# Window attention with its gradients: the order of products in a pair of tiles, and the shape of the first scores

## The chip, the cores and the metric

The kernel runs on one core of a Trainium2 chip. The metric is the device time of one execution in microseconds; smaller is better. PE is the matrix engine, DVE the vector engine, ACT the scalar engine, POOL and SP two more engines that here only issue transfers (DMA).

## The reference

The input is an image of 256 x 256 positions with C = 384 channels, cut into 32 x 32 windows of 8 x 8 = 64 positions. Attention is done inside each window, with one head, and a vector-Jacobian product follows:

```python
qkv = xw @ wqkv                       # xw: 1024 windows x 64 x 384
p = softmax(einsum('bqc,bkc->bqk', q, k) * C ** -0.5)
o = einsum('bqk,bkc->bqc', p, v) @ wo
# outputs: o, and the gradients of x, wqkv and wo for a given grad_out
```

All is bfloat16 in memory. The outputs are `out_0` (o), `out_1` (gradient of x), `out_2` and `out_3` (gradients of the weights).

## The kernel before, in words

The weights are folded once at the start into four 384 x 384 matrices, so that the scores and their gradient, and all that follows, are products with x and grad_out directly. A *tile* is 16 x 8 positions, two windows one above the other, 128 rows for the 128 partitions. Four tiles make a *quad*; there are 128 quads, and a call of `step` works on three of them at once: c (the one before), b (this one) and a (the next one).

Accumulators of PE live in one ring of eight slots (`ring`, 8 banks of 128 x 384 or 128 x 512 float32). Each new accumulator takes the slot of the one eight before it, and its first product waits until that slot has been emptied by a copy or an addition on ACT or DVE. The one exception is the scores' tile `sd`, which is held longer. Slots are handed out in the order in which the code asks for them, and the order of instructions on every engine is the order of the code: nothing is rescheduled. The waits are set by the framework from the tiles.

What a step puts on PE, in order:

1. `scores` of b (sd, 24 products of 128 x 128 weights by 64 columns, through `product`, L146).
2. `uv` of b: eight accumulators pj of three products each (128x128 by 384 columns, L146), copied by ACT (L228).
3. `project` kind 0 of a: three accumulators pj of three products (128x128 by 512 columns, L146), copied by ACT (L160).
4. One accumulator pg of a gradient of the weights (`filler(1)`, `gf_group`, twelve products by 384 columns), which DVE adds to `GF_acc` (L289). The products are there from the time that three quads are done.
5. `attend` of c for the tiles 2 and 3, then `turn` of b (pt: eight products of 128 x 64 weights by 128 columns, L234, copied by DVE at L237).
6. `project` kind 1 of a and one more pg, both in column halves: with `split[0]` set, `product` makes two products of 128x64 (L144) that run side by side, one to the lower and one to the upper 64 partitions.
7. `attend` of b for the tiles 0 and 1.

`attend` takes a *pair* of tiles. For each tile it has four accumulators: po (the output), pu and pw (for the gradients of the weights) and pd (gradient of x). `both` makes four 64x64 products for two of these accumulators, which run side by side on the four quarters of the array (L256): first a group of four for pu and po, then a group for pw and pd. So a pair has four groups. After them come, for each tile, two *token products* into pd (K = 128, 128x64 by 384 columns, L271), which use the transposed projections `tok`. po is copied by ACT to osb (L263), pu and pw by DVE to Uq and Wq (L264, L266), and pd by ACT to dsb (L274). `store` issues two transfers per result on POOL's queue (L246). POOL's queue also issues the loads of grad_out (dq, L118), SP's queue the loads of x (xq, L117) and the three transposing transfers of a quad (dT and xT at L127, tok at L166). The loads are issued three quads ahead, the transposes into dT and xT two.

Of the kernel before, what the change touches and what calls it, by code (L numbers as in the profile page):

```python
# [12 lines left out]
F32 = mybir.dt.float32  # L13

P = 128
# [7 lines left out]
def kernel(  # L23
# [21 lines left out]
    nc = tc.nc  # L45
    _, H, W, C = x.shape
# [13 lines left out]
    ring = ctx.enter_context(tc.tile_pool(name="ring", bufs=8, space=bass.MemoryType.PSUM))  # L60
# [26 lines left out]
    for dst, left, lo, right, ro, sc in (  # L87
# [5 lines left out]
        for mr in range(CK):  # L93
            pc = ring.tile([P, C], F32, tag="r")
            for mc in range(CK):
                nc.tensor.matmul(pc[:], lhsT=left[:, lo + mc, mr * P:(mr + 1) * P], rhs=right[:, ro + mc, :],  # L96
                                 start=(mc == 0), stop=(mc == CK - 1))
# [8 lines left out]
    def dram_tile(ap, bp, t):  # L106
        return ap[0, 2 * WIN * bp:2 * WIN * (bp + 1), WIN * t:WIN * (t + 1), :]

    LO, HI = slice(0, WT), slice(WT, P)
# [29 lines left out]
    split = [ALL]  # L139

    def product(out, lhsT, rhs, start, stop):
        if split[0]:
            for h in (LO, HI):
                nc.tensor.matmul(out[h], lhsT=lhsT[:, h], rhs=rhs, start=start, stop=stop)  # L144
        else:
            nc.tensor.matmul(out, lhsT=lhsT, rhs=rhs, start=start, stop=stop)  # L146

    ENG = {"D": nc.vector.tensor_copy, "A": nc.scalar.copy}
# [20 lines left out]
    def scores(st):  # L169
        yz, xT = st["yz"], st["xT"]  # L170
        st["sd"] = sd = ring.tile([P, QUAD, 2, WT], F32, tag="r", name="sd")
        for t in range(QUAD):
            for w in range(2):
                for m in range(CK):
                    product(sd[:, t, w, :], yz[:, m, t, 2 * w:2 * w + 2, :].rearrange("p s k -> p (s k)"),
                            xT[:, t, m, w * WT:(w + 1) * WT], m == 0, m == CK - 1)
# [53 lines left out]
    def turn(st):  # L230
        pt = ring.tile([P, QUAD, 2, WT], F32, tag="r", name="pt")
        for t in range(QUAD):
            for w, h in ((0, LO), (1, HI)):
                nc.tensor.matmul(pt[h, t, :, :].rearrange("p s k -> p (s k)"), lhsT=st["ps"][:, w, t, :],  # L234
                                 rhs=ident[:], start=True, stop=True)
        st["PS"] = dst = qp.tile([P, QUAD, 2, WT], BF16, tag="PS", name="PS")
        nc.vector.tensor_copy(out=dst[:], in_=pt[:])  # L237

    def turned(st, n, t, h):
        if n in ("PT", "ST"):  # L240
            return st["PS"][h, t, int((n == "ST") == (h == LO)), :]
        return st[n][h, t, :]

    def store(dst, src, bp, t):
        for h, w in ((LO, 1), (HI, 0)):
            nc.gpsimd.dma_start(out=dram_tile(dst, bp, t)[WIN * w:WIN * (w + 1)], in_=src[h, :])  # L246

    def attend(st, pair, after=None):
        bp, t0 = st["at"]
        if pair[0] == 0:  # L250
            st["Uq"] = grp.tile([P, QUAD, C], BF16, tag="Uq", name="Uq")
            st["Wq"] = grp.tile([P, QUAD, C], BF16, tag="Wq", name="Wq")
        def both(straight, crossed):
            for h, o, (dst, lhs, rhs, done) in ((LO, LO, straight), (LO, HI, crossed), (HI, LO, crossed),
                                                (HI, HI, straight)):
                nc.tensor.matmul(dst[o, :], lhsT=turned(st, lhs, t, h), rhs=st[rhs][h, t, :], start=True, stop=done)  # L256

        made = []
        for t in pair:
            po, pu, pw, pd = [ring.tile([P, C], F32, tag="r", name=n) for n in ("po", "pu", "pw", "pd")]  # L260
            both((pu, "ST", "xq", True), (po, "PT", "uq", True))
            osb = ob.tile([P, C], BF16, tag="o")
            ENG[EV["o"][t]](out=osb[:], in_=po[:])  # L263
            ENG[EV["U"][t]](out=st["Uq"][:, t, :], in_=pu[:])  # L264
            both((pw, "Pb", "dq", True), (pd, "ST", "vq", False))
            ENG[EV["W"][t]](out=st["Wq"][:, t, :], in_=pw[:])  # L266
            made.append((t, pd))
            store(out_0, osb, bp, t0 + t)
        for t, pd in made:
            for w, o in ((0, HI), (1, LO)):  # L270
                nc.tensor.matmul(pd[o, :], lhsT=st["ps"][:, w, t, :], rhs=st["tok"][:, :, t, w, :], start=False,  # L271
                                 stop=True)
            dsb = ob.tile([P, C], BF16, tag="d")
            ENG[EV["d"][t]](out=dsb[:], in_=pd[:])  # L274
            store(out_1, dsb, bp, t0 + t)
        if after is not None:
            turn(after)
# [22 lines left out]
    def step(c, b, a):  # L300


        def on(st):
            return (lambda f, *r: f(st, *r)) if st is not None else (lambda f, *r: None)
        C_, B, A = on(c), on(b), on(a)
        B(scores)
        B(soft, 0)
        B(uv, 0, 0)
# [17 lines left out]
        if c is not None:  # L326
            attend(c, (2, 3), b)
        else:
            B(turn)
# [4 lines left out]
        filler(1)  # L334
        split[0] = ALL
        B(attend, (0, 1))

    G_ON_PE = 0
    EV = {"z": "AAA", "y": "AAA", "u": "AAAA", "v": "AAAA", "o": "AAAA", "U": "DDDD", "W": "DDDD", "d": "AAAA"}
    quads = [(bp, t0) for bp in range(NBP) for t0 in range(0, NT, QUAD)]  # L340
    sts = [{"at": q, "i": i} for i, q in enumerate(quads)]
    n = len(sts)
# [33 lines left out]
    for ma in range(CK):  # L376
        for i, (lhs, f, rhs, r0) in enumerate(((GFT, 0, w_sb, C), (GFb, 0, w_sb, 0), (GFT, 1, woT_sb, 0))):
            pe = ring.tile([P, C], F32, tag="r")
            for mb in range(CK):
                nc.tensor.matmul(pe[:], lhsT=lhs[:, f, mb, ma * P:(ma + 1) * P], rhs=rhs[:, mb, r0:r0 + C],  # L380
                                 start=(mb == 0), stop=(mb == CK - 1))
# [6 lines left out]
    for mc in range(CK):  # L388
        pe = ring.tile([P, C], F32, tag="r")
        for ma in range(CK):  # L390
            nc.tensor.matmul(pe[:], lhsT=w_sb[:, ma, 2 * C + mc * P:2 * C + (mc + 1) * P], rhs=GFb[:, 1, ma, :],
                             start=(ma == 0), stop=(ma == CK - 1))
# [32 lines left out]
```

## Time and profile before

| what | value |
|---|---|
| median of four runs | 2046.67 us |
| lowest and highest run | 2041.24, 2060.6 us |
| the profiled execution | 2041.24 us, its span 2039.5 us |
| mean granted PE clock | 0.999 |
| copy of po on ACT (L263), mean | 483 ns, 512 of them |
| copy of pd on ACT (L274), mean | 483 ns, 512 of them |
| copies of pu and pw on DVE (L264, L266), mean | 547 and 546 ns, 512 each |
| addition of pg on DVE (L289), mean | 557 ns, 258 of them |
| issue of a store on POOL (L246), mean | 570 and 563 ns, 1024 of each output |
| stores, issue to landing | 4.7 us, median |

A line of a group reads: line of the source, engine, operation, destination and sources, tile shape of the weights (rows*columns), shape of the moving operand, count. In the timeline the first two columns are start and duration in microseconds; instructions of a kind that follow each other are merged, with their number at the end (x8), and brackets tell the idle time before and what ended it. PE's durations run past the start of the next product, because products are pipelined.

### The profile page before, as it was taken

The page shows a single profiled execution, that of the slowest core. Times are in us where ns is not written, and L with a number is a line of the kernel's source. Part 1 is how long each engine was busy: PE and PEld are TensorE (multiplying, and loading weights), DVE is VectorE, ACT ScalarE, POOL GpSimd, SP SyncE. Part 2 cuts the span into 40 slices and gives each one's busy share as a digit, 9 for nine tenths or more (in the row PEclk, how much of TensorE's full clock was granted, in tenths as well). Part 3 has the DMA queues.
Part 4 walks back from the last instruction along what each step waited for, and adds up shares of the span by engine and source line. Part 5 has one row for each costly group of instructions (what it writes and reads, how often), then busy time and mean ns, then how long its engine had stood idle before and what let it go on. Part 6 is the DMA issues. An engine that isn't in the chain of part 4 may idle for free.

```text
span 2039.5 us, 54462 instructions
## 1 busy us (share of the span) xinstructions
PE 2021.9 (99%) x20442; PEld 1146.7 (56%) x20442; DVE 1382.2 (68%) x3107; ACT 1469.3 (72%) x3213; POOL 1419.2 (70%) x2566
## 2 busy tenths in 40 slices
PE   8999999999999999999999999999999999999998
PEld 4455555555555555555555555555555555555555
DVE  5666666666666676666666666666666667666665
ACT  6777777777777777777777777777777777777773
POOL 4766777677666777677676677767666777776764
PEclk9999999999999999999999999999999999999999
DMA  9999999999999999999999999999999999999992
GB/s 208 223 209 198 212 201 203 209 200 213 196 204 194 209 204 212 202 204 202 203 209 200 199 208 202 205 205 202 196 198 213 200 204 202 211 197 204 205 181 79
DMA packets 997192, 409.25 MB, mean 201 GB/s; under 512 B 880704, under 2 KB 971584, under 8 KB 996928
## 3 DMA queue, kind: packets, MB, share of 16 engines
q1 hardware_dynamic: 873648, 253.80, 76.1%
q0 software_dynamic: 122880, 151.68, 31.7%
q8 instruction: 159, 2.61, 0.6%
q14 instruction: 105, 0.86, 0.2%
q10 hardware_dynamic: 400, 0.29, 0.0%
HBM read 101.84 MB, written 101.84 MB: 100 GB/s over the span
## 4 chain that ended last, share of the span: by engine, by line
PE 97%; DMA 1%; DVE 1%; ACT 1%; POOL 0%; issue 0%; POOLq 0%
PE pj L146 36%; PE pg L146 12%; PE pj L144 12%; PE pg L144 12%; PE pd L271 6%; PE pu L256 5%; PE sd L146 5%; PE pw L256 4%; PE pd L256 3%; PE pt L234 1%; DMA dT<-dq 0%; PE pc L96 0%; DMA out_dram<-osb 0%; DMA w_sb<-in_wqkv_dram 0%; PE pe L380 0%
## 5 line engine op out<-in xcount | busy, mean ns | idle before, releaser
L246 POOL DMA_DIRECT2D out_dram<-osb x1024 | 577.1, 570 | 341.5 <-ACT osb L263 145.2
L246 POOL DMA_DIRECT2D out_dram<-dsb x1024 | 571.2, 563 | 207.6 <-DMA dq<-in_grad_out_dram 60.9
L289 DVE TENSOR_TENSOR GF_acc<-pg,GF_acc 128x384 f32<-128x384 f32 x258 | 143.7, 557 | 460.8 <-PE pg L144 316.6
L146 PEld LDWEIGHTS <-xT 128*128 128x128 bf16 x3072 | 291.8, 98 | 182.2
L263 ACT CAST osb<-po 128x384 bf16<-128x384 f32 x512 | 220.9, 483 | 232.6 <-PE pu L256 175.0
L146 PE MATMUL pj<-B_sb,xT 128*128 128x384 bf16 x1536 | 333.4, 326 | 0.0
L146 PE MATMUL pj<-AT_sb,xT 128*128 128x384 bf16 x1536 | 333.3, 326 | 0.0
L118 POOL DMA_DIRECT2D dq<-in_grad_out_dram x512 | 274.1, 550 | 50.2 <-DMA out_dram<-osb 19.4
L228 ACT CAST uq<-pj 128x384 bf16<-128x384 f32 x512 | 247.4, 483 | 73.6 <-PE pj L146 69.4
L264 DVE CAST Uq<-pu 128x384 bf16<-128x384 f32 x512 | 280.0, 547 | 9.5 <-PE pu L256 6.1
L266 DVE CAST Wq<-pw 128x384 bf16<-128x384 f32 x512 | 279.8, 546 | 0.0
L146 PE MATMUL pj<-dT,BT_sb 128*128 128x512 bf16 x1152 | 270.8, 380 | 2.2 <-DMA dT<-dq 2.2
L144 PE MATMUL pj<-xT,A_sb 128*64 128x512 bf16 x2304 | 270.0, 379 | 0.0
L228 ACT CAST vq<-pj 128x384 bf16<-128x384 f32 x512 | 250.1, 489 | 2.4
L274 ACT CAST dsb<-pd 128x384 bf16<-128x384 f32 x512 | 221.2, 483 | 37.7 <-DMA out_dram<-dsb 1.9
L162 ACT CAST yz<-pj 128x512 bf16<-128x512 f32 x384 | 224.6, 586 | 32.0 <-PE pj L144 0.2
L256 PE MATMUL pw<-dq,Pb 64*64 64x384 bf16 x1024 | 228.4, 329 | 0.3
L144 PEld LDWEIGHTS <-xq 128*64 128x64 bf16 x3000 | 170.1, 110 | 86.6
L146 PEld LDWEIGHTS <-xq 128*128 128x128 bf16 x1572 | 153.7, 98 | 115.1 <-issue 0.6
L256 PEld LDWEIGHTS <-PS 64*64 64x64 bf16 x3072 | 120.2, 105 | 163.0 <-issue 150.3
L206 ACT COPY ps<-Pb 64x256 bf16<-64x256 bf16 x256 | 103.2, 403 | 149.6 <-DVE Pb L203 148.1
L160 ACT CAST yz<-pj 128x512 bf16<-128x512 f32 x384 | 206.6, 644 | 2.1 <-PE pj L146 2.0
(64 smaller groups left out, 2720.4 us busy)
## 6 DMA issues: line engine op xcount, KB each, us to landing
xq<-in_x_dram SPq DMA_DIRECT2D x512, 96.0 KB, 4.1
dq<-in_grad_out_dram POOLq DMA_DIRECT2D x512, 96.0 KB, 5.3
out_dram<-osb POOLq DMA_DIRECT2D x1024, 48.0 KB, 4.7
out_dram<-dsb POOLq DMA_DIRECT2D x1024, 48.0 KB, 4.7
dT<-dq SPq DMA_TRANSPOSE x128, 6.0
xT<-xq SPq DMA_TRANSPOSE x128, 7.7
tok<-yz SPq DMA_TRANSPOSE x128, 8.7
w_sb<-in_wqkv_dram SPq DMA_DIRECT2D x1, 864.0 KB, 5.5
```

The costliest lines, as they stand in the source:

```text
L118: nc.gpsimd.dma_start(out=dq[:, t, :], in_=dram_tile(grad_out, bp, t0 + t))
L144: nc.tensor.matmul(out[h], lhsT=lhsT[:, h], rhs=rhs, start=start, stop=stop)
L146: nc.tensor.matmul(out, lhsT=lhsT, rhs=rhs, start=start, stop=stop)
L160: ENG[EV["z"][mo]](out=yz[:, mo, :, 0:4:3, :], in_=pj[:])
L162: ENG[EV["y"][mo]](out=yz[:, mo, :, 1:3, :], in_=pj[:])
L228: cp(out=dst[:, t, :], in_=pj[:])
L246: nc.gpsimd.dma_start(out=dram_tile(dst, bp, t)[WIN * w:WIN * (w + 1)], in_=src[h, :])
L256: nc.tensor.matmul(dst[o, :], lhsT=turned(st, lhs, t, h), rhs=st[rhs][h, t, :], start=True, stop=done)
L263: ENG[EV["o"][t]](out=osb[:], in_=po[:])
L264: ENG[EV["U"][t]](out=st["Uq"][:, t, :], in_=pu[:])
L266: ENG[EV["W"][t]](out=st["Wq"][:, t, :], in_=pw[:])
L274: ENG[EV["d"][t]](out=dsb[:], in_=pd[:])
```

## The change

The token products of both tiles of a pair now come first, ahead of all four groups. They open pd (`start=True`), and the 64x64 products add to it (`start=False`) and close it. The accumulators are taken in another order: po of the first tile, pd of both tiles, pu, pw, then po, pu, pw of the second tile; before, it was po, pu, pw, pd for one tile and then for the other. ACT copies po of the first tile, then pd of both, and po of the second tile last. All stores of a pair are issued after the last copy, in the same order as before. And the first of the eight score products of a quad (tile 0, window 0) is made in column halves: six products of 128x64 in place of three of 128x128.

```diff
@@ scores
             for w in range(2):
+                split[0] = t == 0 and w == 0
                 for m in range(CK):
                     product(sd[:, t, w, :], yz[:, m, t, 2 * w:2 * w + 2, :].rearrange("p s k -> p (s k)"),
                             xT[:, t, m, w * WT:(w + 1) * WT], m == 0, m == CK - 1)
@@ attend
-                nc.tensor.matmul(dst[o, :], lhsT=turned(st, lhs, t, h), rhs=st[rhs][h, t, :], start=True, stop=done)
-
-        made = []
+                nc.tensor.matmul(dst[o, :], lhsT=turned(st, lhs, t, h), rhs=st[rhs][h, t, :], start=dst not in pds,
+                                 stop=done)
+
+        osbs, pds = [], []
         for t in pair:
-            po, pu, pw, pd = [ring.tile([P, C], F32, tag="r", name=n) for n in ("po", "pu", "pw", "pd")]
+            po = ring.tile([P, C], F32, tag="r", name="po")
+            if t == pair[0]:
+                pds = [ring.tile([P, C], F32, tag="r", name="pd") for _ in pair]
+                for u, pd in zip(pair, pds):
+                    for w, o in ((0, HI), (1, LO)):
+                        nc.tensor.matmul(pd[o, :], lhsT=st["ps"][:, w, u, :], rhs=st["tok"][:, :, u, w, :], start=True,
+                                         stop=False)
+            pd = pds[t - pair[0]]
+            pu = ring.tile([P, C], F32, tag="r", name="pu")
             both((pu, "ST", "xq", True), (po, "PT", "uq", True))
             osb = ob.tile([P, C], BF16, tag="o")
-            ENG[EV["o"][t]](out=osb[:], in_=po[:])
+            osbs.append((t, po, osb))
+            if t == pair[0]:
+                ENG[EV["o"][t]](out=osb[:], in_=po[:])
             ENG[EV["U"][t]](out=st["Uq"][:, t, :], in_=pu[:])
-            both((pw, "Pb", "dq", True), (pd, "ST", "vq", False))
+            pw = ring.tile([P, C], F32, tag="r", name="pw")
+            both((pw, "Pb", "dq", True), (pd, "ST", "vq", True))
             ENG[EV["W"][t]](out=st["Wq"][:, t, :], in_=pw[:])
-            made.append((t, pd))
-            store(out_0, osb, bp, t0 + t)
-        for t, pd in made:
-            for w, o in ((0, HI), (1, LO)):
-                nc.tensor.matmul(pd[o, :], lhsT=st["ps"][:, w, t, :], rhs=st["tok"][:, :, t, w, :], start=False,
-                                 stop=True)
+        dsbs = []
+        for t, pd in zip(pair, pds):
             dsb = ob.tile([P, C], BF16, tag="d")
             ENG[EV["d"][t]](out=dsb[:], in_=pd[:])
+            dsbs.append((t, dsb))
+        t, po, osb = osbs[1]
+        ENG[EV["o"][t]](out=osb[:], in_=po[:])
+        for t, po, osb in osbs:
+            store(out_0, osb, bp, t0 + t)
+        for t, dsb in dsbs:
             store(out_1, dsb, bp, t0 + t)
```

## The prediction

> **What bounds the kernel now.** First the page's busy times and its chain of work that ended last: which engine sets the end.
>
> ```profile
> PE 2021.9 (99%) x20442; PEld 1146.7 (56%) x20442; DVE 1382.2 (68%) x3107; ACT 1469.3 (72%) x3213; POOL 1419.2 (70%) x2566
> PE 97%; DMA 1%; DVE 1%; ACT 1%; POOL 0%; issue 0%; POOLq 0%
> ```
>
> PE is the path; every other engine is idle for a quarter of the span or more. But a PE shown busy is not a PE streaming all the time: a matmul's shown duration (326 ns for 384 columns) is about twice its spacing (0.163 us in a run of equals), so pauses of 0.1 to 0.2 us between starts hide inside it. So next I read the timeline and compare start times. One pair of tiles, the last of a quad (the copies of tile 1 and the output stores are cut):
>
> ```profile
> 1008.43 2.12 PE L144 MATMUL pg<-Wq,xq 128*64 128x384 bf16 x24
> 1010.48 0.35 PE L256 MATMUL pu<-xq,PS 64*64 64x384 bf16 x1
> ...
> 1010.59 0.56 DVE L289 TENSOR_TENSOR GF_acc<-pg,GF_acc 128x384 f32<-128x384 f32 x1 [2.56 <-PE pg L144]
> 1010.66 0.32 PE L256 MATMUL pw<-dq,Pb 64*64 64x384 bf16 x1
> ...
> 1010.83 0.32 PE L256 MATMUL pu<-xq,PS 64*64 64x384 bf16 x1
> ...
> 1010.92 0.86 ACT L263 CAST osb<-po 128x384 bf16<-128x384 f32 x2 [1.69 <-PE pu L256]
> 1010.99 0.32 PE L256 MATMUL pw<-dq,Pb 64*64 64x384 bf16 x1
> ...
> 1011.21 0.35 PE L256 MATMUL pd<-vq,PS 64*64 64x384 bf16 x2
> ...
> 1011.49 0.52 PE L271 MATMUL pd<-tok,ps 128*64 128x384 bf16 x4
> ...
> 1011.94 0.87 PE L146 MATMUL sd<-xT,yz 128*128 128x64 bf16 x24
> ...
> 1012.65 0.49 PE L146 MATMUL pj<-B_sb,xT 128*128 128x384 bf16 x2
> ```
>
> Columns: start, duration, engine, line. Read three things. (1) The four groups of 64x64 products start at 1010.48, .66, .83 and .99, that is 0.18, 0.17, 0.16 apart. The fourth breaks: its first product runs at 1010.99, the other three at 1011.21. They write pd of the second tile, the eighth accumulator after pg in a ring of eight, so they wait for the DVE add that empties pg: 1010.59 + 0.56 = 1011.15, and PE goes on 0.06 later. The hole is 0.21 us. (2) Each change of the tile shape costs about 0.095: the last pg pair starts at 1008.43 + 11 x 0.163 = 1010.22, the next group 0.26 later instead of 0.163. Tokens to sd: 0.45 for two token pairs (0.19 + 0.16 without a change) and one change. (3) The copy of po starts 0.44 after its group (1010.48 to 1010.92), since ACT is idle then.
>
> The other pair of the quad is the same up to the tokens; pt follows them in the same shape:
>
> ```profile
> 1005.92 0.52 PE L271 MATMUL pd<-tok,ps 128*64 128x384 bf16 x4
> ...
> 1006.26 0.39 PE L234 MATMUL pt<-ident,ps 128*64 128x128 bf16 x8
> ...
> 1006.49 2.11 PE L144 MATMUL pj<-xT,A_sb 128*64 128x512 bf16 x18
> ```
>
> Tokens to pt takes 0.34 us; pt's four pairs of 128x64 take 0.23, so 0.055 a pair. Last, how fast ACT's end releases PE, from a place near the start where PE waits for it, and how long the copy of po is:
>
> ```profile
> 19.76 1.88 ACT L162 CAST yz<-pj 128x512 bf16<-128x512 f32 x3 [0.19 <-PE pj L144]
> ...
> 21.70 0.81 PE L146 MATMUL sd<-xT,yz 128*128 128x64 bf16 x22 [0.44 <-ACT yz L162]
> ...
> L263 ACT CAST osb<-po 128x384 bf16<-128x384 f32 x512 | 220.9, 483 | 232.6 <-PE pu L256 175.0
> ```
>
> 19.76 + 1.88 = 21.64, and sd goes on at 21.70: 0.06 after ACT's end, as after DVE's. A quad's period is 15.62 us, and 128 of them are 1999 of the 2039.5.
>
> **The change part by part**, per quad, along PE. G is the start of the first 64x64 group of a pair.
>
> Removed: the wait for the pg add. With tokens first, the ring gives pg's slot to pw of the second tile, again in the fourth group. That group now comes later after pg. In pair (0,1): tokens 0.16 after the last pg pair (no change of shape), 0.16 for the second pair, 0.26 with a change to the groups: G = pg + 0.58, fourth group at G + 0.51 = pg + 1.09. The add frees the slot at pg + 0.37 + 0.56 + 0.06 = pg + 0.99. In pair (2,3) a change lies before the tokens, G = pg + 0.26 + 0.19 + 0.26 = pg + 0.71, and the margin is larger. So the hole of 0.21 goes, twice: -0.42 to -0.43. The margin may even be lost: late by another 0.18 it would hide behind the next wait.
>
> Added, a wait: what is late next is po. Accumulators are now taken as po, pd, pd, pu, pw, po, pu, pw; the ninth (pt after pair (2,3), sd after pair (0,1)) takes the slot of the first po, as it did before. Before, the tokens (0.34) stood between the groups and the ninth. Now it follows directly. Without a wait it would start at G + 0.51 + 0.28 (the fourth group to the next shape, 1011.21 to 1011.49) = G + 0.79 to 0.80. The copy of po starts at G + 0.44, lasts 0.48, releases PE 0.06 later: G + 0.98. So PE waits 0.18, twice: +0.36. Behind the waiting matmul stand pt's and project's products (or all scores, u and v) on PE; nothing passes them. DVE sees scores and ACT sees pj that much later, but both are idle at points in the period.
>
> Added, one change of shape: before, pg(128x128), groups, tokens and pt(128x64), pg, groups, tokens, sd(128x128) make five changes. Now pg(128x128), tokens, groups, pt, pg and tokens, groups, sd halves, sd full make six. +0.095 to 0.10 from row (2).
>
> Split scores: three products of 64 columns, 0.029 each (24 take 0.71), become three concurrent pairs of 128x64. The trace has no such product with 64 columns. Lower end: 0.029 a pair, so no cost but start-up 0.02. Upper end: the weight load of that shape (LDWEIGHTS 128*64, 0.11) unhidden once per pair. Nearest is pt, the same shape with its loads hidden, 0.055 a pair; I take that: 3 x (0.055 - 0.029) = +0.08, less 0.03 because the tokens of pair (0,1) no longer open a shape and so lose their slow first pair: +0.05. By the ends it is -0.03 to +0.21.
>
> The Trainium skill speaks against this part: TensorEngine Tiling (Array Packing), Restrictions, says column tiling shuts off the fast weight load, and TensorE: Matmul & The Clock Gate puts a plain load at columns / 1.2, here 53 ns for 64. Two loads in turn would be 0.107 a pair, three pairs +0.16 us a quad over my value, about 20 us in all, an estimate from those pages; pt's 0.055 a pair shows that the two loads do not queue up there.
>
> Moved at no cost: the copies on ACT go po, pd, pd, po. The second po copy ends near G + 2.05 (0.44, then three starts 0.38 apart, 0.86 - 0.48 from the row, then 0.48); its slot is wanted by v of the third tile some 4 us after G or, in the other pair, by the tokens 4 us on. The pd copies end at G + 1.3 and G + 1.7, wanted at G + 1.9 (second pj of project) and G + 3.1 (pg). The eight stores of a pair now stand on POOL's queue after all four copies: the first still has its data at G + 0.92, and two stores take 2 x 0.57 us, so the second tile's data is there when its store's turn comes; POOL is busy 70%, the dq loads behind are issued three quads ahead. SP's queue is not passed by anything. Softmax: the chain on DVE starts after the same four copies, some 0.2 us later against PE; in the next period its last step ended at 1019.53 and the pt that needs it ran at 1021.88. The token transposes that the first tokens need are issued a quad earlier (8.7 us to land, 15.6 there).
>
> Sum: -0.43 + 0.36 + 0.10 + 0.05 = +0.08 us a quad, x 128 = +10.2 us. Seven pairs at the start have no pg product before them and so no hole to lose: + 7 x 0.21 = 1.5. Total +11.7. The profiled execution took 2041.24 us, so **2053 us**. That execution is the fastest of four (median 2046.67, up to 2060.6), so against the median this is +0.3%, and a change under about 1% can't be told from none here.
>
> **The rivals.** *No new wait (faster).* If the copy of po released its slot by G + 0.80, both waits fall away: -0.36 x 128 = -46, so 2007 us. For it: ACT's second copy starts 0.38 after the first, before the first's 0.48 are over, so the shown duration might overstate. Against it: 21.64 to 21.70, PE went on only after ACT's shown end. It would have to release 0.18 earlier; it decides (over 1% faster) from 0.13.
>
> *The halves don't hide their weights (slower).* Six loads of 0.11 in turn instead of 0.165 for all: +0.50 x 128 = +63, so 2116; with one load per pair exposed, +0.16 x 128 = +21, 2074. It decides from about 0.08 us a quad above my sum, a pair at 0.08 instead of 0.055. For it: the load stands behind a matmul that waits, so nothing is loaded ahead. Against it: pt's rate.
>
> *The old wait stays.* If the pg add releases the fourth group later than pg + 1.09, nothing happens until it is 0.18 late, since the po copy covers it; beyond that each 0.1 us is 26 us. DVE is idle 2.56 us before the add, so I give it little.
>
> **How the numbers follow.** The sum's case 0.72, own range 2040 to 2062 (2043 by the halves' lower end, 2 to 5 us for the spread of the runs on either side; the upper end takes part of the halves' cost). No new wait 0.12, unhidden halves 0.11, others 0.05. Low 2036 and high 2068 leave out most of both rivals, about 2 in 10. Faster by over 1% is the first rival: 0.12. Slower by over 1%: 0.14, the second and a part of the rest. Same: 0.74.
>
> **What would show it.** In the changed timeline, no break inside the fourth group; pt and sd start at G + 0.98, not G + 0.80, 0.06 after the end of the first po copy; tokens 0.26 behind pg in pair (2,3), 0.16 in pair (0,1); the three pairs of halves take 0.165. The period is 15.70 instead of 15.62. I'm wrong if pt starts at G + 0.80, if the halves take 0.3, or if PE shows a wait that I costed at nothing.

## The result

The changed kernel takes 2054.41 us (median of 43 runs, 2050.65 to 2063.59), the kernel before 2047.61 us (64 runs, 2040.35 to 2060.6). The ratio is 1.0032, interval 1.0023 to 1.0041: slower by 0.3%, which so many runs do tell from no change. The profiled executions' spans are 2048.9 and 2039.5 us, 9.4 us apart; the prediction had +11.7. All ratios leave out executions over 1.5% above the fastest of the same kernel (one of the kernel before, two of the third order below); medians and ranges have them.

First the chain of work that ended last, from the changed kernel's page.

```profile
PE 69%; ACT 14%; DMA 6%; issue 5%; POOL 3%; DVE 0%; POOLq 0%; SPq 0%
```

ACT is on the chain now, with 14%, where it had 1%. Its place is seen in the changed kernel's timeline of a pair (0,1):

```profile
1013.24 2.15 PE L144 MATMUL pg<-Wq,xq 128*64 128x384 bf16 x24
...
1015.19 0.52 PE L267 MATMUL pd<-tok,ps 128*64 128x384 bf16 x4
1015.42 0.56 DVE L304 TENSOR_TENSOR GF_acc<-pg,GF_acc 128x384 f32<-128x384 f32 x1 [2.34 <-PE pg L144]
...
1015.64 0.35 PE L257 MATMUL pu<-xq,PS 64*64 64x384 bf16 x1
...
1016.08 0.48 ACT L275 CAST osb<-po 128x384 bf16<-128x384 f32 x1 [2.03 <-PE pu L257]
1016.15 0.32 PE L257 MATMUL pw<-dq,Pb 64*64 64x384 bf16 x1
1016.15 0.33 PE L257 MATMUL pd<-vq,PS 64*64 64x384 bf16 x2
...
1016.61 0.28 PE L144 MATMUL sd<-xT,yz 128*64 128x64 bf16 x6
1016.83 0.79 PE L146 MATMUL sd<-xT,yz 128*128 128x64 bf16 x21
...
1017.45 0.65 PE L146 MATMUL pj<-B_sb,xT 128*128 128x384 bf16 x3
```

The fourth group (1016.15, both lines) has no break: pw and pd start together. The addition ends at 1015.98, 0.17 before the group. The first copy of po ends at 1016.08 + 0.48 = 1016.56, and the scores start at 1016.61: G + 0.97, 0.05 after the copy. The other pair of the quad, again of the changed kernel:

```profile
1007.62 2.11 PE L146 MATMUL pg<-Wq,xq 128*128 128x384 bf16 x12
...
1009.66 0.52 PE L267 MATMUL pd<-tok,ps 128*64 128x384 bf16 x4
...
1010.10 0.35 PE L257 MATMUL pu<-xq,PS 64*64 64x384 bf16 x1
...
1010.55 0.48 ACT L275 CAST osb<-po 128x384 bf16<-128x384 f32 x1 [0.61 <-ACT yz L160]
...
1011.08 0.41 PE L235 MATMUL pt<-ident,ps 128*64 128x128 bf16 x8
...
1011.30 2.14 PE L144 MATMUL pj<-xT,A_sb 128*64 128x512 bf16 x18
```

pt starts at G + 0.98, 0.05 after the copy's end at 1011.03. Most of these two stops is not shown as a wait of PE for ACT: by the groups, PE is idle 19.1 us before pt and 16.9 before the halves in the whole span, of some 51 us that 2 x 127 stops of 0.20 (first experiment) make; the durations of the matmuls before cover the rest. Only 3.3 us of the idle time is put down to osb, 8 waits of 0.4. The stops must be read from the starts.

The *period* below is the time from a quad's first score product to the next quad's, median of the 127 in a trace. It is 15.619 us before and 15.680 after. Before, 122 of them lie within 0.01 of that; after, 114 do, and eight, every sixteenth, take 0.28 more. They fit the 8 waits above: in one of them the groups start where they do in the quad before it, but the copy of po that pt waits for starts 0.28 later. What holds ACT there isn't known; half stores (below) leave these periods as they are.

### The profile page after: what moved, and what is told of

It reads as the page before. It is cut to its first block, busy times and chain, and to the rows that moved or that the text cites. A ratio compares the mean times of both kernels' runs of the same rounds, so it can differ in the third digit from the quotient of the medians.

```text
span 2048.9 us, 54585 instructions
## 1 busy us (share of the span) xinstructions
PE 1995.6 (97%) x20826; PEld 1233.3 (60%) x20826; DVE 1405.8 (69%) x3107; ACT 1446.2 (71%) x3213; POOL 1419.0 (69%) x2566
## 4 chain that ended last, share of the span: by engine, by line
PE 69%; ACT 14%; DMA 6%; issue 5%; POOL 3%; DVE 0%; POOLq 0%; SPq 0%
PE pj L146 33%; PE pg L144 10%; PE pj L144 10%; ACT yz L160 8%; ACT osb L275 6%; PE pg L146 5%; PE sd L146 4%; POOL out_dram L247 2%; PE pt L235 2%; DMA out_dram<-dsb 2%; PE pu L257 2%; PE pd L267 2%; DMA out_dram<-osb 2%; DMA dq<-in_grad_out_dram 2%; PE sd L144 2%
## 5 line engine op out<-in xcount | busy, mean ns | idle before, releaser
L275 ACT CAST osb<-po 128x384 bf16<-128x384 f32 x256 | 122.6, 479 | 333.8 <-PE pu L257 225.8
L144 PEld LDWEIGHTS <-xq 128*64 128x64 bf16 x3000 | 210.8, 110 | 46.3 <-issue 0.3
L144 PEld LDWEIGHTS <-A_sb 128*64 128x64 bf16 x2304 | 150.3, 110 | 68.5 <-issue 0.4
L146 PEld LDWEIGHTS <-BT_sb 128*128 128x128 bf16 x1152 | 112.6, 98 | 122.8 <-DMA dT<-dq 0.8
```

## The experiments

**One wait or one part at a time.** Four kernels, all against the kernel before.

The changed kernel, the first copy no longer reading po:

```diff
             if t == pair[0]:
-                ENG[EV["o"][t]](out=osb[:], in_=po[:])
+                ENG[EV["o"][t]](out=osb[:], in_=st["uq"][:, t, :])
```

> The changed kernel, but the ACT copy of the first tile of a pair reads uq (in SBUF) in place of po, so that po's slot is free as soon as PE has written it. It leaves out the copy of half of out_0. My account (the stop before pt and sd is a wait for this copy, 0.18 us twice a quad): pt and sd start at G + 0.80 in place of G + 0.98 (G: first 64x64 group of the pair), 46 us less, about 2008 us, ratio to the kernel before 0.981. Rival (the 0.45 us from the last group to pt or sd is what the change of shape and the weight load behind it cost there): pt and sd stay at G + 0.98 and the time at 2054.

Measured: 2044.25 us (10 runs, 2034.55 to 2057.56), ratio 0.9984, interval 0.9956 to 1.0012. Its timeline, one pair of each kind:

```profile
1611.65 0.35 PE L257 MATMUL pu<-xq,PS 64*64 64x384 bf16 x1
...
1612.42 0.41 PE L235 MATMUL pt<-ident,ps 128*64 128x128 bf16 x8
1612.69 2.13 PE L144 MATMUL pj<-xT,A_sb 128*64 128x512 bf16 x18
...
1617.03 0.35 PE L257 MATMUL pu<-xq,PS 64*64 64x384 bf16 x1
...
1617.81 0.28 PE L144 MATMUL sd<-xT,yz 128*64 128x64 bf16 x6
```

pt and sd start at G + 0.77 and G + 0.78: the stop was the wait for the copy, and the rival (change of shape and weight load) falls. Each stop was 0.20, so 0.40 a quad; but pt, which no longer waits, takes 0.27 to the next product (1612.42 to 1612.69) where it took 0.22 (1011.08 to 1011.30). Why it does isn't shown. The period is 15.329, 0.351 less. But the time went down by 10 us, not 46. The gain was given back in some periods: one in ten took 16.47 or more, the longest 21.2. So a second question came up: what makes periods late.

The kernel before, the addition no longer reading pg:

```diff
-                nc.vector.tensor_tensor(out=GF_acc[:, f, ma, :], in0=pw[:], in1=GF_acc[:, f, ma, :], op=ALU.add)
+                nc.vector.tensor_tensor(out=GF_acc[:, f, ma, :], in0=st["xq"][:, 0, :], in1=GF_acc[:, f, ma, :], op=ALU.add)
```

> The kernel before, but the DVE addition reads xq (in SBUF) in place of pg, so that pg's slot is free as soon as PE has written it; the sums of the weights' gradients are left out. My account (the hole in the fourth group is the wait for this addition): no hole, 0.21 us less in 249 pairs, 53 us less, about 1994 us, ratio 0.974. Rival (the hole is PE's own, a weight load that comes late in the fourth group): the hole stays, 2047.

Measured: 2062.05 us (10 runs, 2050.7 to 2073.01), ratio 1.0079, interval 1.005 to 1.0108: slower, where both theories had faster or equal. Yet the hole is gone, as its timeline shows:

```profile
1742.61 0.35 PE L256 MATMUL pu<-xq,PS 64*64 64x384 bf16 x1
...
1743.12 0.32 PE L256 MATMUL pw<-dq,Pb 64*64 64x384 bf16 x1
1743.13 0.33 PE L256 MATMUL pd<-vq,PS 64*64 64x384 bf16 x2
...
1743.39 0.52 PE L271 MATMUL pd<-tok,ps 128*64 128x384 bf16 x4
```

The fourth group is whole, the tokens come at G + 0.78 in place of G + 1.01. The period's median is 15.156, 0.46 less, but a quarter of the periods took 16.23 or more.

The changed kernel without the split scores:

```diff
-                split[0] = t == 0 and w == 0
```

> The changed kernel without its second part: all scores are 128x128 products. My account: the copy of po still holds sd back until G + 0.98, the change of shape from 64x64 to 128x128 is over by then, and 24 whole products take 0.71 us in place of the 0.84 from the first half to the end of the scores: 0.13 x 128 = 17 us less than the changed kernel, about 2037 us, ratio to the kernel before 0.995. Rival (the halves spare a dear change straight from 64x64 to 128x128): not faster than the changed kernel, 2054 or more.

Measured: 2041.28 us (10 runs, 2035.94 to 2049.3), ratio 0.9965, interval 0.9938 to 0.9993. Its timeline:

```profile
1614.36 0.35 PE L256 MATMUL pu<-xq,PS 64*64 64x384 bf16 x1
...
1615.33 0.86 PE L146 MATMUL sd<-xT,yz 128*128 128x64 bf16 x24
1616.03 0.65 PE L146 MATMUL pj<-B_sb,xT 128*128 128x384 bf16 x3
```

The scores start at G + 0.97 as with halves, though the shape goes straight from 64x64 to 128x128, and end 0.70 later in place of 0.84. The period is 15.539, 0.141 less than with halves. The halves bring nothing here: the change of shape that they put off lies inside the wait for po. Without them the new order is no slower than the old one (0.9965).

A third order, tokens of the first tile ahead of the groups, those of the second behind them, whole scores (`tokens` makes the two token products of a tile, `finish` copies its pd):

```diff
         for t in pair:
+            first = t == pair[0]
+            if first:
+                pd = ring.tile([P, C], F32, tag="r", name="pd")
+                tokens(pd, t, True)
...
+            if not first:
+                tokens(pd, t, False)
+                made.append((t, finish(pd, t)))
```

> A third order: the token products of the first tile ahead of the groups, those of the second tile behind them, all scores 128x128. My account: the fourth group starts 0.93 to 1.03 us after pg (free at 0.98), so the old hole is 0.05 at most, and pt and sd come 0.98 to 1.13 after G, when po is copied; against the kernel before 0.17 us less in pair (0,1) and 0.09 less in pair (2,3), 33 us less, about 2015 us, ratio 0.984. Rival (what counts is the number of changes of shape, six as in the changed kernel): 2054 or little less.

Measured: 2041.29 us (10 runs, 2023.32 to 2071.42), ratio 0.9954, interval 0.9917 to 0.9992. The order does on PE what was expected, also in the profiled execution, which is the longest of the ten:

```profile
1761.54 0.35 PE L256 MATMUL pu<-xq,PS 64*64 64x384 bf16 x1
...
1762.05 0.32 PE L256 MATMUL pw<-dq,Pb 64*64 64x384 bf16 x1
1762.10 0.35 PE L256 MATMUL pd<-vq,PS 64*64 64x384 bf16 x2
...
1762.38 0.35 PE L260 MATMUL pd<-tok,ps 128*64 128x384 bf16 x2
1762.66 0.87 PE L146 MATMUL sd<-xT,yz 128*128 128x64 bf16 x24
```

The hole is 0.05 (1762.05 to 1762.10), the scores start at G + 1.12, no wait for po. The period is 15.380, 0.239 less than before (0.26 expected), with six changes of shape a quad; so it is not their number that counts. 0.239 x 128 is 31 us, and 6 came out in the medians. Again a part of the periods is late.

**What makes periods late.** In the first experiment the longest one reads so (ACT and PE, idle time in brackets):

```profile
1050.15 0.48 ACT L283 CAST dsb<-pd 128x384 bf16<-128x384 f32 x1 [7.15 <-DMA out_dram<-dsb]
...
1050.68 1.12 PE L146 MATMUL pj<-AT_sb,xT 128*128 128x384 bf16 x3 [4.39 <-ACT dsb L283]
```

By the profile a store of dsb hadn't landed, the copy into that buffer waited 7.15 us for it, and PE waited 4.39 for the copy. In all, ACT's copies of pd waited so:

```profile
ACT dsb L283 <- DMA out_dram<-dsb: 103.9, 81, 7.1
```

In the changed kernel itself this sum is 0.4 us, once. Two explanations: too few store buffers, or transfers that can't keep up. Four kernels were to tell them apart. *More buffers*, in three kernels, six per output in place of four, with four scratch tiles of the softmax at one buffer in place of two to make room:

```diff
-    ob = ctx.enter_context(tc.tile_pool(name="ob", bufs=4))
+    ob = ctx.enter_context(tc.tile_pool(name="ob", bufs=6))
```

The split-token order:

> The split-token order with six store buffers per output in place of four (four scratch tiles of the softmax have one buffer in place of two to make room). Without late periods PE's 15.38 us a quad gives about 2015 us. If the late periods come from too few store buffers (ACT's copy waits for a store, PE for the copy): late periods all but gone, 2012 to 2022, spread of runs a few us. If the transfers themselves can't keep up with a quad in 15.38 us: the same as with four, about 2041, spread 20 us and more.

Measured: 2087.53 us (4 runs, 2083.55 to 2091.19), ratio 1.0201, interval 1.0169 to 1.0233.

The changed kernel with po unread:

> The changed kernel whose first copy reads uq in place of po (half of out_0 is not the copy of po), now with six store buffers. The period without late ones was 15.33 us. If the buffers are the second limit: about 2008 us. If the transfers are: about 2044 as with four.

Measured: 2092.26 us (4 runs, 2076.81 to 2105.45), ratio 1.0215, interval 1.0155 to 1.0275.

The changed kernel with whole scores:

> The changed kernel with whole scores only and six store buffers. The period without late ones was 15.54 us. If the buffers are the second limit: about 2036 us, its spread no more than 5 us. If the transfers are: 2041 as with four.

Measured: 2092.99 us (4 runs, 2081.74 to 2100.83), ratio 1.0218, interval 1.0174 to 1.0261.

All three are 2% slower than the kernel before, which neither explanation had. More buffers don't help: ACT's copies of pd still wait for stores, 120.2 us in the split-token order (135.0 with four buffers) and 187.0 with po unread (103.9). And transfers got slower, as the issues of the first of these show (size, then median from issue to landing):

```profile
dq<-in_grad_out_dram POOLq DMA_DIRECT2D x512, 96.0 KB, 6.9
...
tok<-yz SPq DMA_TRANSPOSE x128, 10.9
```

In the kernel before these took 5.3 and 8.7, in the split-token order with four buffers 5.6 and 10.0. Whether the six buffers did it, by more stores in flight, or the scratch tiles, wasn't separated.

*Less to transfer*: stores of half the columns, as many as before:

```diff
-            nc.gpsimd.dma_start(out=dram_tile(dst, bp, t)[WIN * w:WIN * (w + 1)], in_=src[h, :])
+            nc.gpsimd.dma_start(out=dram_tile(dst, bp, t)[WIN * w:WIN * (w + 1), :, :C // 2], in_=src[h, :C // 2])
```

With the split-token order:

> The split-token order with stores of half the columns: the other half of out_0 and out_1 is never written; the number of stores stays. If the load on the transfers is the second limit: late periods gone, 2015 us. If it is the number of stores and the order in which POOL issues them (0.57 us each, and a wait for the eighth one before): late periods stay, about 2035 to 2041. If it is the number of store buffers: between, since a shorter store frees its buffer sooner.

Measured: 2011.39 us (4 runs, 2010.24 to 2012.22), ratio 0.9823, interval 0.9799 to 0.9847. The late periods are gone: the median is 15.378 and 95 in 100 are at most 15.38. The number of stores is what it was, and an issue on POOL takes 568 and 561 ns where it took 570 and 563, so it is not POOL's issue of them. What makes stores land late isn't separated further: the bytes themselves, or POOL's queue, where in the program each transfer waits until the eighth before it has landed. Fewer bytes shorten that wait too: POOL's stores waited 190.4 us for loads of dq in the split-token order and 35.5 with half stores. Then the same for the kernels whose sums the prediction had made:

> The kernel before with stores of half the columns (half of out_0 and out_1 is never written). If PE's path sets the time of the kernel before, as predicted: its period stays at 15.62 us and the time within 8 us of the kernel before, at the low end of its runs, about 2040 us. If the transfers set it: clearly less, 2020 or below.

Measured: 2039.52 us (10 runs, 2038.49 to 2042.55), ratio to the kernel before with whole stores 0.9968, interval 0.9952 to 0.9984.

> The changed kernel with stores of half the columns (half of out_0 and out_1 is never written). PE's path: period 15.68, about 9 us over the kernel before with half stores, 2050 us. Transfers: 2030 or below.

Measured: 2050.45 us (10 runs, 2048.05 to 2053.42), ratio 1.0012, interval 0.9998 to 1.0026.

> The changed kernel with half stores, and the first copy of a pair reads uq in place of po (half of out_0 and out_1 is never written, and half of what is written of out_0 is no copy of po). With the transfers out of the way my account of the wait for po shows in the time: 0.35 x 128 = 45 us less than the changed kernel with half stores, about 2005 us. Rival (the period's gain is given back elsewhere than at the transfers): 2030 to 2044, as with whole stores.

Measured: 2004.82 us (4 runs, 2000.48 to 2007.47), ratio 0.9786, interval 0.9757 to 0.9814.

> The kernel before with half stores, and the addition reads xq in place of pg (half of out_0 and out_1 is never written, the weights' gradients are not summed). My account of the hole, by the period of 15.155 seen with whole stores: 0.21 to 0.23 x 249 = 53 to 58 us less than the kernel before with half stores, about 1985 us. Rival as above: 2030 or more.

Measured: 1980.01 us (4 runs, 1979.14 to 1981.26), ratio 0.9667, interval 0.9642 to 0.9693.

Together, in us:

| kernel | period, whole stores | time | period, half stores | time |
|---|---|---|---|---|
| before | 15.619 | 2047 | 15.619 | 2039.5 |
| changed | 15.680 | 2054 | 15.680 | 2050.5 |
| changed, po unread | 15.329 | 2044 | 15.329 | 2004.8 |
| before, pg unread | 15.156 | 2062 | 15.154 | 1980.0 |
| split tokens | 15.380 | 2041 | 15.378 | 2011.4 |

PE's own period doesn't depend on the stores; whether the time follows it does. With half stores all five times follow the period (each is 40 to 44 us over 128 of them). With whole stores only those do whose period is about 15.6, to within 8 us; below that, transfers come late and hold PE up. The share of the transfer engines in the changed kernel with po unread, with half stores and then with whole ones (start and end of the stretch, its length, then the engines' busy time; DMA share and GB/s at the end):

```profile
300.00:1900.00 1600.00, 1600.00 (x16933) 981.54 (x16924) 1132.77 (x2503) 1183.39 (x2608) 1155.69 (x2090) 1.00 0.99 182
```

```profile
300.00:1900.00 1600.00, 1573.16 (x16528) 955.99 (x16526) 1107.52 (x2449) 1147.22 (x2552) 1132.22 (x2044) 1.00 1.11 203
```

The share adds up the queues, so over 1 an engine had packets of two of them under way at once. It is 1.11 with whole stores and 0.99 with half; and 27 us of PE's idle time lie in the second stretch, none in the first. The share alone doesn't tell: the kernel before has 1.11 in the same stretch of its profile, at 15.619 and with no idle time of PE, and with half stores and pg unread it is 1.03, again with none.

## Why the prediction was right, step by step

- *The hole.* Put at 0.21, twice a quad. Shown: taken away, it is worth 2039.5 - 1980.0 = 59.5 us with half stores, and by the period 0.46 a quad, so 0.23 each. The 0.02 over is the change of shape behind the group, which is a little cheaper after a group without a break (tokens at G + 0.78, not 0.80).
- *The new wait.* Put at 0.18, twice, from three rows: the copy starts at G + 0.44, lasts 0.48, releases PE 0.06 later. Shown: pt and sd at G + 0.98 and 0.97; taken away, 0.351 a quad and, with half stores, 2050.5 - 2004.8 = 45.6 us for the 46 put. That this agrees so well is partly luck: without the wait pt and sd come at G + 0.77 and 0.78, not 0.80, so the stops are 0.20 each, 0.40 a quad, of which 0.05 comes back because pt then takes longer. The rival that ACT releases early falls.
- *One more change of shape.* Put at 0.095 to 0.10. Tokens start 0.26 after the last pg product in pair (2,3), with a change, and 0.16 in pair (0,1), without one, as put. It wasn't shown alone. Together with the halves it was put at 0.15 and is 0.173: the new order without its wait has a period of 15.329, the old one without its hole 15.156.
- *The halves.* Here a size was off. The pairs were put at 0.055, pt's rate, between 0.029 and 0.11; six halves start within 0.28 - 0.198 = 0.08 us (the row's 0.28 less one product's mean duration), about 0.03 a pair: the lower end. Waiting for po is not what hides the weights: of the six loads only the first starts ahead, at 1016.41, while the other five start at 1016.62 to 1016.67, along with the products; and with po unread, where nothing waits, the halves take the same 0.22 us to the first whole product. By the Trainium skill (TensorE: Matmul & The Clock Gate, LDWEIGHTS) one load of 64 columns takes 64 / 1.2 = 53 ns; two in turn would be 107, an estimate. The trace disagrees with that as a rate, for here the pairs start 0.03 apart, each with its two loads. What I missed is the comparison: the sum priced the halves against whole products, when what matters is that whole scores would have had their change of shape inside the wait. Taking the halves out gives 0.141 a quad.
- *The sum.* Put at +0.08 a quad, shown -0.463 + 0.351 + 0.173 = +0.061; +11.7 us put, 9.4 between the spans, 10.9 between the medians with half stores. Some 2.2 us of these, the eight periods with a late copy (8 x 0.28), were in no term. 2053 lies so near the median of 2054 partly by chance: I added 11.7 to the fastest of four runs, and the medians lie 7 apart. With whole stores the median of the kernel before is some 7 us longer than with half stores (2046.8 to 2039.5), that of the changed kernel, which is slower on PE, some 4. Late transfers are the likely reason; it isn't shown, as the profiled executions, the fastest or nearly the fastest of these two kernels, hardly have any.
- *The rivals.* The second rival (weights unhidden) didn't come; nor did the third: the addition released the fourth group 0.1 ahead of its need.
- *What I didn't see.* The page's share of the two queues, 76.1% and 31.7%, is over 100% together. I read it and left it, since PE's only waits for a transfer were 2.2 us, once, and the loading of the weights at the start. In the changed kernel it costs nothing new, as PE got slower. Had the first rival been right, its 2007 us would have been wrong: it would have been about 2044.

One thing about the ring: in the built programs slots don't go strictly to the accumulator eight places on (some go five, seven, nine or more places on). For pg's slot and for the first po's, on which the sums rest, it comes to the same: pd of the second tile before and its pw after take pg's slot, pt and sd take that of the first po.

## What to carry to other kernels

Before moving work ahead of a wait, ask what that work was covering where it stood: the tokens hid the copy of po, and moved away they traded a hole of 0.21 us for a wait of 0.18 and a change of shape. On an engine shown 99% busy, compare the starts of neighbouring products; a stop of a fifth of a microsecond need not show as idle time. And see how far the next limit is before counting a gain. A queue share over 100% and a spread of runs of 1% hinted that one was near, but not how near. The runs put it 0.1 to 0.2 us a quad away: at 15.619 whole stores cost some 7 us over half ones, at 15.380 some 30, and at 15.539 the time is some 10 us over what the period gives by the half-store kernels.

## What the hardware showed that I had not expected

- Changing straight from 64x64 to 128x128 products behind a wait costs nothing visible: sd starts 0.05 after ACT's end with halves and without.
- The transfers' limit isn't a wall but shows as late periods: with PE's period at 15.156 one period in four was late by 1.1 us or more; at 15.329, one in nine; at 15.539, 5 of 127; at 15.619, none. These are the profiled executions; that at 15.539 is the slowest of its kernel, that at 15.619 among the fastest.
- Halving the bytes of the stores narrows the runs of the kernel before from 2041.6 to 2052.9 (those beside it) to 2038.5 to 2042.6, with the profiled period unchanged. So most of the spread of this kernel's runs goes with the bytes of its stores.
